# Lightning attention and a gated FFN on one core: the order of two transposes, of eight stores and of the state's decay

## The chip, the core and the metric

The kernel runs on one core of a Trainium2 chip. Five engines work side by side: TensorE (PE) does the matrix products, VectorE (DVE) and ScalarE (ACT) the elementwise work, GpSimd (POOL) issues the loads, SyncE (SP) issues the transposing transfers and the stores. Each engine takes its own instructions in order, and semaphores order work between engines. The metric is the device time of one execution in microseconds (us), as the median of seven runs. Beside it stands one execution that the profiler recorded.

## What is computed

Linear attention with a decay per head, over 4 sequences, 8 heads, 768 positions and 64 features, taken block by block; its output is the input of a gated FFN:

```python
for b in range(nb):                      # blocks of the sequence
    intra = einsum('bhic,bhjc->bhij', qb, kb) * Dmask[None]      # lam ** (i - j), lower triangle
    intra = einsum('bhij,bhjd->bhid', intra, vb)
    inter = einsum('bhid,bhde->bhie', qb * lam_pow[None], kv_state)
    out[:, :, sl] = intra + inter
    kb_dec = kb * rev_pow[None]
    kv_state = lam_block * kv_state + einsum('bhsd,bhse->bhde', kb_dec, vb)

x = out.transpose(0, 2, 1, 3).reshape(3072, 512)
y = (sigmoid(x @ w_gate) * (x @ w_val)) @ w_out      # d_ff = 1536
```

Inputs and output are float32; the kernel works in bfloat16 with float32 accumulators.

## The kernel before, in words

**Blocks.** The kernel takes 128 positions at a time: six blocks, n = 0 to 5, each of all 4 sequences and 8 heads. The FFN of a block has 12 tiles of the hidden width. For each tile `piece_gv` (line 488) runs four matmuls of the gate product into `gp` and four of the value product into `vp`, ACT takes the sigmoid of `gp` into `sg` (line 500), and DVE multiplies it with `vp` into `ht` (lines 503 and 505). `gp` and `vp` share three PSUM buffers. After the tiles, `piece_po` (line 522) makes the output rows of the four sequences, ACT copies each to `ob` (line 526), and SP stores it (line 512).

**Attention of the next block.** While the FFN of block n runs, the attention of block nx = n + 1 is prepared between its tiles. The order is written out by hand: `plan` is a list of units, `more[i]` is the list of pieces that follow tile i, and the program's text order is each engine's own order. For nx = 2 and later, the pieces are `e_q` (DVE: q transposed, times its decay, into `QS`, line 277), `chunk_s` (PE: scores, which reads `QS` and the transposed k, line 387), `chunk_m` (DVE: mask, line 397), `kd` (ACT: k times its decay, line 127, four groups of two heads), `decayed` (DVE: the state times its decay, into `XD`, line 456), `chunk_c` (PE: the state's increments from `kd` and v, line 447), `update_0` and `update_1` (DVE, lines 464 and 472), and after the last tile `att` (PE: the block's output, lines 411 and 425). `chunk_c` stands behind tile 8. In the FFN of block 1 most of these stand one tile later than in that of blocks 2 to 4 (`late`).

**Loads and transposes.** `next_loads(n)` has three steps. `xbar(n)` lets SP issue two transposing transfers, from `kb` to `KT` and from `qb` to `QT` (line 298), which wait for the three k loads and the three q loads of the block. `gate(n)` is a pair of tiny copies on POOL (line 615), which read the last elements of `KT` and `QT`, and so hold POOL until both transposes have landed. Then POOL issues v of block n and k and q of block n + 1 (lines 94 and 100), k ahead of q. Blocks 2 and 3 have their calls in the FFN of block 1, behind tiles 2 and 8; those of blocks 4 and 5 stand in the last output unit of blocks 1 and 2. The k and q of block 2 are loaded with blocks 0 and 1's data, before the first call.

**Stores of block 0.** Its output rows are copied to `ob` before block 1's FFN begins, but `piece_po` does not store them (`if n:`). They are stored by eight transfers of half rows that are listed behind a tile of block 1's FFN.

Of the kernel before, what the change touches and what calls it, by code (L numbers as in the profile page):

```python
# [16 lines left out]
def kernel(  # L17
# [242 lines left out]
    QT, KT = {}, {}  # L260
# [32 lines left out]
        nc.vector.tensor_copy(T_[c, 0][:, b], H32[c, b])  # L293

    def xbar(n):
        for c, d in (("k", KT), ("q", QT)):
            d[n] = qtp.tile([128, B, HP, C], BF16, tag=c + "t", name=c + "t")
            nc.sync.dma_start_transpose(  # L298
                out=d[n].rearrange("p b hp s -> p (b hp) s"),
                in_=T_[c, n].rearrange("p b h d -> p (b h d)"))  # L300
        for b in range(B):
            KS[n, b] = KT[n][:, b]
# [208 lines left out]
    def store(n, tt, c0=0, c1=DM):  # L511
        (nc.scalar if (n, tt, c1) == (NSTEP - 1, B - 1, DM) else nc.sync).dma_start(out=out[tt * S + n * C:tt * S + (n + 1) * C, c0:c1],
                          in_=OB[n, tt][:, c0:c1])
# [103 lines left out]
    def next_loads(n):  # L617
        xbar(n)
        gate(n)
        load(n, "v")  # L620
        if n + 1 < NSTEP:
            load(n + 1, "kq")
# [8 lines left out]
    def gv(n, ft, *more):  # L631
        unit(lambda: piece_gv(n, ft), *more)

    def po(n, tt, *more, c=(0, DM), eng=nc.scalar, fts=range(NFT)):
        unit(lambda: piece_po(n, tt, *c, eng, fts), *more)
# [16 lines left out]
    def do(f, *args, **kw):  # L652
        return lambda: f(*args, **kw)
# [4 lines left out]
    def att(n):  # L658
        def block():
            piece_i(n)  # L660
            piece_a(n, range(B))
            piece_x(n, range(B))
            for bp in range(2):
                piece_c(n, bp)

        def chunks():
            new_xt(n)
            for c, bp in A + Z:
                new_op(n, c, bp)
            done = [chunk_i(n, banks) for banks in (A, Z)]  # L670
            for name, banks in zip(done, (A, Z)):
                in_order(name)
                chunk_a(n, banks)
                for c, bp in banks:
                    chunk_x(n, c, bp)
        return block if n < FIRST_XBAR else chunks

    def kd(n, h0, h1=None, **kw):
        return do(piece_kd, n, range(h0, h1 or h0 + 2), **kw)
# [20 lines left out]
    for n in range(1, NSTEP):  # L700
        nx = n + 1
        more = [[] for i in range(NFT)]
        if nx < NSTEP:
            late = 1 if n == 1 else 0
            cs = (0, 1) if nx < NSTEP - 1 else (0,)
            for bp in range(2):
                more[2 + late + bp].append(do(e_q, nx, [2 * bp, 2 * bp + 1]))
                more[4 + late].append(do(chunk_s, nx, bp))
                more[8].append(do(chunk_c, nx, bp, cs))
            for bp in range(2):  # L710
                more[4 + late + bp].append(do(chunk_m, nx, bp))
                more[8].append(do(update_0, nx, bp))
                if 1 in cs:
                    more[9 + bp].append(do(update_1, nx, bp))
            more[6 + late].append(do(decayed, nx))
            more[3 + late].insert(0, do(make_kd, nx))
            for i in range(4):
                more[3 + late + i].append(kd(nx, 2 * i))
            more[11].append(att(nx))
        if n == 1:  # L720
            more[0].append(chunk_lamq)
            more[2].append(lambda: next_loads(2))
            more[3].extend([lambda tt=tt, j=j: store(0, tt, 256 * j, 256 * j + 256)
                            for tt in range(B) for j in range(2)])
            more[8].append(lambda: next_loads(3))
        for ft in range(NFT):
            gv(n, ft, *more[ft])
        for tt in range(B):
            if n == NSTEP - 1 and tt == B - 1:
                po(n, tt, c=(0, 384), eng=nc.vector)  # L730
                po(n, tt, c=(384, 512))
            else:
                more = [lambda n=n: next_loads(n + 3)] if tt == B - 1 and n + 3 < NSTEP else []
                po(n, tt, *more)
# [35 lines left out]
```

## Time and profile before

| | |
|---|---|
| median of 7 runs | 227.17 us (227.04 to 227.89) |
| profiled execution: its time, its span | 227.45 us, 225.7 us |
| granted TensorE clock | 1.0 of full speed |
| busy: TensorE, its weight loads | 216.2 us, 105.9 us |
| busy: VectorE, ScalarE, GpSimd | 104.2 us, 106.4 us, 63.9 us |
| FFN products: gate, value, output | 74.2 us (296 recorded), 74.1 us (292), 63.3 us (292) |
| transposes of k and of q, issue to landing | 4.5 to 6.5 us, 4.7 to 4.9 us (four of each) |
| v loads of 512 KB, issue to landing | 8.6, 8.0, 7.3 and 6.9 us (blocks 2 to 5) |

How to read it. The span runs from the first to the last recorded event of the profiled execution; its own time is 1.75 us longer. Busy time is the time in which an engine works on an instruction; waiting on a semaphore is not in it. The chain that ended last starts from the last instruction and goes back, at each step, to what released it or to the instruction before it on its engine: it is the list of things that set the end. The list of waits tells which engine waited at which line for whom. For a transfer the profile has two times: the interval in which an engine or a queue issues it, and the time from issue to landing. Numbers behind an L are line numbers of the kernel.

### The profile page before, as it was taken

How to read it: one execution, taken by the hardware profiler on the slowest of the kernel's cores; microseconds unless marked ns; L12 is line 12 of the kernel's file. 1: busy time of each engine (PE TensorE's matmuls, PEld its weight loads, DVE VectorE, ACT ScalarE, POOL GpSimd, SP SyncE). 2: the span in 40 equal slices, each digit the busy share in tenths (PEclk: the TensorE clock that was granted, in tenths of full speed). 3: DMA queues.
4: the chain of work that ended last, by engine and by line, in shares of the span. 5: the costliest groups of instructions: out<-in, count | busy, mean ns of one | idle time of the engine just before them, and what ended most of it. 6: DMA issues, size and time to landing. Idle time of an engine off the chain costs nothing.

```text
span 225.7 us, 5200 instructions
## 1 busy us (share of the span) xinstructions
PE 216.2 (96%) x2178; PEld 105.9 (47%) x2187; DVE 104.2 (46%) x196; ACT 106.4 (47%) x232; POOL 63.9 (28%) x83
## 2 busy tenths in 40 slices
PE   7699999999997999999999999999999999999994
PEld 2454444557443544444544444544444454444443
DVE  4785553539478800478800378800378500333300
ACT  5777534494374342385342385342385342333221
POOL 7998855660085008400930030000000000000000
PEclk9999999999999999999999999999999999999999
DMA  7999999999989998998999839012100012100022
GB/s 113 149 161 184 196 203 180 172 154 137 169 196 166 141 206 99 208 166 144 74 157 195 178 62 90 3 49 93 46 3 0 0 52 94 46 0 0 4 93 94
DMA packets 106008, 25.25 MB, mean 112 GB/s; under 512 B 97152, under 2 KB 103552, under 8 KB 105984
## 3 DMA queue, kind: packets, MB, share of 16 engines
q0 software_dynamic: 82944, 13.90, 86.0%
q1 hardware_dynamic: 22752, 10.95, 20.2%
q8 instruction: 17, 0.28, 0.5%
q10 hardware_dynamic: 288, 0.07, 0.1%
q14 instruction: 7, 0.06, 0.1%
HBM read 28.32 MB, written 6.29 MB: 153 GB/s over the span
## 4 chain that ended last, share of the span: by engine, by line
PE 67%; DMA 23%; POOL 6%; issue 2%; SPq 1%; ACT 0%; POOLq 0%
PE po L522 23%; PE gp L488 20%; PE vp L488 20%; DMA WO<-in_moe_w_out_dram 6%; DMA kb<-in_k_dram 4%; DMA vb<-in_v_dram 4%; DMA WV<-in_moe_w_val_dram 4%; DMA WG<-in_moe_w_gate_dram 3%; DMA qt<-qb 2%; SPq L298 1%; POOL vb L94 1%; PE cp L447 1%; PE op L411 1%; PE op L425 1%; POOL WG L105 1%
## 5 line engine op out<-in xcount | busy, mean ns | idle before, releaser
L488 PE MATMUL gp<-XT,WG 128*128 128x512 bf16 (+1 forms) x296 | 74.2, 374 | 0.2 <-DMA WG<-in_moe_w_gate_dram 0.2
L488 PE MATMUL vp<-XT,WV 128*128 128x512 bf16 (+1 forms) x292 | 74.1, 376 | 0.0
L500 ACT ACTIVATE sg<-gp 128x512 bf16<-128x512 f32 x72 | 43.0, 597 | 64.8 <-PE gp L488 61.4
L505 DVE TENSOR_TENSOR ht<-sg,vp 128x512 bf16<-128x512 bf16 x48 | 33.0, 687 | 79.9 <-PE vp L488 79.9
L522 PE MATMUL po<-WO,ht 128*128 128x512 bf16 (+2 forms) x292 | 63.3, 370 | 0.5 <-issue 0.2
L488 PEld LDWEIGHTS <-WV 128*128 128x128 bf16 x292 | 28.6, 98 | 33.4
L522 PEld LDWEIGHTS <-ht 128*128 128x128 bf16 x300 | 28.3, 98 | 31.9
L488 PEld LDWEIGHTS <-WG 128*128 128x128 bf16 x296 | 28.1, 98 | 32.1 <-DMA WG<-in_moe_w_gate_dram 0.9
L526 ACT COPY ob<-po 128x512 f32<-128x512 f32 (+1 forms) x24 | 13.7, 572 | 38.9 <-PE po L522 38.9
L127 ACT ACTIVATE kd<-kb,kds 128x128 bf16<-128x128 bf16 (+1 forms) x88 | 28.8, 401 | 0.0
L503 DVE TENSOR_TENSOR ht<-sg,vp 128x512 bf16<-128x512 bf16 x24 | 16.5, 686 | 13.0 <-PE vp L488 13.0
L615 POOL COPY gates<-kt 128x1 bf16<-128x1 bf16 x4 | 0.7, 186 | 51.2 <-DMA kt<-kb 51.2
L94 POOL DMA_DIRECT2D vb<-in_v_dram x9 | 11.9, 1332 | 2.6 <-issue 1.7
L318 DVE TENSOR_TENSOR MT<-sp,mask 128x512 bf16<-128x512 f32 x16 | 9.9, 684 | 3.0 <-PE sp L310 3.0
L437 ACT CAST XT<-op 128x512 bf16<-128x512 f32 x16 | 8.2, 599 | 5.0 <-PE op L425 5.0
L397 DVE TENSOR_TENSOR MT<-sp,mask 128x512 bf16<-128x512 f32 x16 | 10.3, 682 | 0.0
L100 POOL DMA_DIRECT2D qb<-in_q_dram x10 | 8.9, 911 | 2.5 <-DMA WO<-in_moe_w_out_dram 2.5
L100 POOL DMA_DIRECT2D kb<-in_k_dram x10 | 8.8, 894 | 1.9 <-DMA WO<-in_moe_w_out_dram 0.7
L94 POOL DMA_DIRECT2D qb<-in_q_dram x8 | 9.0, 1125 | 1.1 <-POOLq L754 0.8
L536 PE MATMUL zps<-st 128*128 128x512 bf16 x17 | 6.4, 509 | 1.6 <-DVE st L159 1.5
L94 POOL DMA_DIRECT2D kb<-in_k_dram x6 | 6.9, 1158 | 1.6 <-DMA WO<-in_moe_w_out_dram 1.1
L108 POOL DMA_DIRECT2D WV<-in_moe_w_val_dram x9 | 6.9, 766 | 1.0 <-DMA WG<-in_moe_w_gate_dram 0.6
(81 smaller groups left out, 114.2 us busy)
## 6 DMA issues: line engine op xcount, KB each, us to landing
out_dram<-ob SPq DMA_DIRECT2D x19, 256.0 KB, 2.1
vb<-in_v_dram POOLq DMA_DIRECT2D x4, 512.0 KB, 7.6
qb<-in_q_dram POOLq DMA_DIRECT2D x6, 256.0 KB, 10.1
kb<-in_k_dram POOLq DMA_DIRECT2D x6, 256.0 KB, 8.3
qb<-in_q_dram POOLq DMA_DIRECT2D x12, 128.0 KB, 9.4
WO<-in_moe_w_out_dram POOLq DMA_DIRECT2D x4, 384.0 KB, 12.3
kb<-in_k_dram POOLq DMA_DIRECT2D x10, 128.0 KB, 9.6
WG<-in_moe_w_gate_dram POOLq DMA_DIRECT2D x4, 256.0 KB, 7.4
```

What stands on the lines that cost most here:

```text
L94: nc.gpsimd.dma_start(out=T_[c, n][:, b0:nat], in_=src[b0:nat, :, sl, :].rearrange("b h s d -> s (b h) d"))
L100: nc.gpsimd.dma_start(out=T_[c, n][:, m:b1, u::2, :], in_=src[m:b1, 1 - u::2, sl, :].rearrange("b h s d -> s (b h) d"))
L127: nc.scalar.mul(KD[n][:, at, i, :], T_["k", n][:, at, i, :], kds[:, min(n // FIRST_XBAR, 1), h:h + 1])
L318: nc.vector.tensor_tensor(out=MT[n, b][:, u], in0=SP[n, b][u], in1=mask0[:, 1 - u if swapped(n, b) else u], op=ALU.mult)
L397: nc.vector.tensor_tensor(out=MT[n, bp][:, u], in0=SP[n, bp][u], in1=mask[:, u ^ bp].unsqueeze(1).to_broadcast([128, 2, HP, L]), op=ALU.mult)
L437: nc.scalar.copy(XT[n][:, c, :, bp * C:(bp + 1) * C], OP[n, c, bp].rearrange("p h j i -> p h (j i)"))
L488: nc.tensor.matmul(ps[:, part], lhsT=W[:, mt, fs], rhs=XT[n][:, part, mt], start=(part is not second and mt == 0), stop=(part is not first ...
L500: nc.scalar.activation(sg, gp.rearrange("p a b -> p (a b)"), AF.Sigmoid)
L503: nc.vector.tensor_mul(HT[n, ft], sg, vp.rearrange("p a b -> p (a b)"))
L505: nc.vector.tensor_mul(HT[n, ft].rearrange("p (b c i) -> p c b i", b=B, c=2), sg.rearrange("p (c b i) -> p c b i", c=2, b=B), vp.rearrange ...
L522: nc.tensor.matmul(po[:, :c1 - c0], lhsT=HT[n, ft][:, tt * 128:(tt + 1) * 128], rhs=WO[:, ft, c0:c1], start=(ft == 0), stop=(ft == NFT - 1))
L526: (eng.copy if eng is nc.scalar else eng.tensor_copy)(o, po[:, :c1 - c0])
```

## The change

Three edits, all to the order of things; no instruction is added or removed.

1. `xbar` issues the transpose of q before that of k, in each of the four blocks that use it. The gate copies and the loads keep their order.
2. The eight stores of block 0 move from the list behind tile 3 of block 1's FFN to that behind tile 6.
3. `decayed` moves from behind tile 6 to behind tile 0 in the FFN of blocks 2 to 4, and from behind tile 7 to behind tile 2 in that of block 1. `make_kd` and the four `kd` groups, which stood behind tiles 3 to 6 in blocks 2 to 4 and behind tiles 4 to 7 in block 1, now stand behind tiles 4 to 7 in all of them.

```diff
     def xbar(n):
-        for c, d in (("k", KT), ("q", QT)):
+        for c, d in (("q", QT), ("k", KT)):
             d[n] = qtp.tile([128, B, HP, C], BF16, tag=c + "t", name=c + "t")
             nc.sync.dma_start_transpose(
...
             late = 1 if n == 1 else 0
             cs = (0, 1) if nx < NSTEP - 1 else (0,)
+            more[2 * late].append(do(decayed, nx))
             for bp in range(2):
                 more[2 + late + bp].append(do(e_q, nx, [2 * bp, 2 * bp + 1]))
                 more[4 + late].append(do(chunk_s, nx, bp))
...
-            more[6 + late].append(do(decayed, nx))
-            more[3 + late].insert(0, do(make_kd, nx))
+            more[4].insert(0, do(make_kd, nx))
             for i in range(4):
-                more[3 + late + i].append(kd(nx, 2 * i))
+                more[4 + i].append(kd(nx, 2 * i))
             more[11].append(att(nx))
         if n == 1:
             more[0].append(chunk_lamq)
             more[2].append(lambda: next_loads(2))
-            more[3].extend([lambda tt=tt, j=j: store(0, tt, 256 * j, 256 * j + 256)
+            more[6].extend([lambda tt=tt, j=j: store(0, tt, 256 * j, 256 * j + 256)
                             for tt in range(B) for j in range(2)])
             more[8].append(lambda: next_loads(3))
```

## The prediction, made blind

> **What bounds the kernel now.** I read the page's busy time first, then the chain that ended last, then the waits, and last the timelines of SP, POOL, DVE and PE around the one place where the chain leaves TensorE. Busy time and the chain's shares on the page:
>
> ```profile
> PE 216.2 (96%) x2178; PEld 105.9 (47%) x2187; DVE 104.2 (46%) x196; ACT 106.4 (47%) x232; POOL 63.9 (28%) x83
> ...
> PE 67%; DMA 23%; POOL 6%; issue 2%; SPq 1%; ACT 0%; POOLq 0%
> ```
>
> TensorE is busy nearly throughout, so only a step that makes it wait longer or shorter moves the end. In order of time the chain runs over DMAs up to 71.9 us, and from there to the end over PE without a gap (columns: start us, length us, what):
>
> ```profile
> 44.84 9.78 DMA kb<-in_k_dram
> ...
> 54.71 3.29 SPq L298
> ...
> 58.10 4.69 DMA qt<-qb
> ...
> 62.84 0.19 POOL gates L615
> ...
> 63.28 8.62 DMA vb<-in_v_dram
> ...
> 71.95 0.73 PE cp L447 x61
> ```
>
> This is block 2's preparation: its k lands at 54.62, SP issues k's transpose and then q's, q's lands at 62.79, the gate copies on POOL let v's load go at 63.28, and v lands at 71.91, where PE stands before chunk_c (line 447). The waits say what PE loses in block 1's FFN (us in total, times, longest):
>
> ```profile
> PE cp L447 <- DMA vb<-in_v_dram: 1.4, 1, 1.4
> PE sp L387 <- DVE QS L277: 0.4, 1, 0.4
> ```
>
> So the v wait ends last: whatever delays v's landing delays the end one for one. SP's timeline shows the transposes and stores:
>
> ```profile
> 54.71 3.29 SPq L298 DMA_TRANSPOSE kt<-kb  x1
> 58.10 3.06 SPq L298 DMA_TRANSPOSE qt<-qb  x1
> 61.22 4.01 SPq L512 DMA_DIRECT2D out_dram<-ob  x8
> ...
> 124.86 1.98 SPq L298 DMA_TRANSPOSE kt<-kb  x1
> 127.07 2.10 SPq L298 DMA_TRANSPOSE qt<-qb  x1
> ```
>
> The last pair (block 5) runs with no load in flight, the first beside q's loads. And POOL's timeline, when block 2's q is loaded and the gates pass:
>
> ```profile
> 46.98 1.76 POOL L100 DMA_DIRECT2D qb<-in_q_dram  x2
> 61.31 0.19 POOL L615 COPY gates<-kt 128x1 bf16<-128x1 bf16 x1 [12.58 <-DMA kt<-kb]
> 62.84 0.19 POOL L615 COPY gates<-qt 128x1 bf16<-128x1 bf16 x1 [1.35 <-DMA qt<-qb]
> ```
>
> **What the Trainium skill says.** "DMA: Bandwidth & Descriptors", section "Issuing engines are not separate DMA queues": transfers issued from different engines run on the same DMA engines and interleave. The trace agrees: a 512 KB v load takes 8.6 us beside the eight stores (block 2) and 6.9 us alone (block 5). The same page, "Latency and other measured facts", gives a DMA transpose 261 GB/s; block 2's transposes move 128 x 2048 x 2 bytes = 524 KB each, an estimate of 2.0 us. Undisturbed, block 5's 1.98 and 2.10 us of issue agree; beside loads the trace has 3.3. "Perfetto Trace Analysis", section "DMA Instruction — HWDGE (DVE, Sync)": the profile's interval of such an instruction is not the data's movement. Here too: q's transpose is issued in 3.06 us but lands after 4.69, so I count landings.
>
> **The change, part by part.**
>
> *Stores of block 0, moved from the list behind FFN tile 3 to that behind tile 6.* I compared the order of instructions on each engine in both kernels. On SP the eight stores still stand between block 2's two transposes and block 3's; SP executes in its own order, and nothing that it issues lies between tiles 3 and 6. Their waits are on the same engines and lanes. Cost 0, as nothing moves. If they did come behind v's load, v could come nearer to its 7.3 us of block 4, 1.3 us of gain; I give that little chance.
>
> *q's transpose ahead of k's, in each block.* POOL loads k and then q, so SP now waits for q first. q's last load is the second of the pair at 46.98: issued at 46.98 + 0.88 = 47.86, and the DMA view gives 9.9 us to landing: 57.7. k's landed at 54.62. So the first transpose starts at 57.8 (0.09 after the landing, as k's did) and not at 54.71: 3.1 late. Part comes back. From the first start to the second landing, the pair took 8.1 us in block 2 (54.71 to 62.79), 8.0 in block 3 (76.81 to 79.89 + 4.9) and 8.3 in block 4 (98.19 to 101.65 + 4.8), each beside q loads still in flight; in block 5, with none, 6.9 (124.86 to 127.07 + 4.7). The swapped pair starts when the loads are over, so I take 6.9 and keep 8.1 as the other end: k's transpose lands at 57.8 + 6.9 = 64.7, against 62.79 before. Gates: k's copy waits for the last landing and q's runs behind it, so 0.2 us is added to the 0.49 from landing to v's issue: v goes at 65.4, against 63.28. Stores: SP is through with the pair after 127.07 + 2.10 - 124.86 = 4.3 us, so they go at 62.1 to 66.1, and cover 0.7 us of v's load instead of 65.23 - 63.28 = 1.95. v took 8.6 with them, 8.0 in block 3 with part of block 1's stores, 7.3 in block 4 and 6.9 with nothing beside; I take 8.2. v lands at 65.4 + 8.2 = 73.6, against 71.91: **+1.7 us**. The ends: 57.8 + 6.9 + 0.5 + 6.9 = 72.1 (+0.2), and 57.8 + 8.1 + 0.7 + 8.6 = 75.2 (+3.3).
>
> What queues behind this on the other engines: DVE's e_q needs only qt, which lands at about 62.4 (57.8 + 4.6), no later than 62.79; so DVE is not held longer. chunk_s on PE needs kt, at 64.7. PE is through with tile 5 at 63.9, waits 0.8 to 0.9 us, but no longer 0.4 for the second QS: it reaches chunk_c some 0.3 us later, at 70.9, and waits there until 73.6, 2.7 us instead of 1.4. The early wait is inside the v delay and is not added.
>
> Later blocks are covered. Block 3's q lands near 79.5 (its last load at 69.85 plus 9.5) against k's 76.8: with POOL's 2 us of lateness the pair starts at 81.6 and lands by 89.7 even at 8.1; v(3) goes at 90.4 and lands at 98.4 with 8.0 us. It is needed by chunk_c at 105.9 + 1.7, and the transposes by e_q at 95.6 + 1.7: 6 us or more of cover. Blocks 4 and 5 have more: their pairs landed at 106.5 and 131.8 for e_q's at about 129 and 163. If a cover were gone, the cost would be the whole lateness, 2 to 5 us a block. Stores of blocks 1 and 2 queue on SP behind these transposes, a few us late, for buffers that are wanted a block (34 us) later.
>
> *State decay (decayed, line 456) from tile 6 to tile 0, in block 1 from tile 7 to tile 2.* One instruction of 1.22 us per block, four in all, same count. In the FFN of blocks 2 to 4 the new place is between ht of tile 0 and of tile 1 (in block 1 between tiles 2 and 3), where DVE waits 1.04 us for PE: the next ht comes at most 0.2 late, and the accumulator that it frees is wanted by the gate product two tiles on, 1 us later. The old place also made PE wait nowhere: the chain runs over gp and vp rows of 0.86 us without a gap. Gain 0, cost 0, as slack covers both.
>
> *k's decay (kd) from tiles 3 to 6 to tiles 4 to 7, in the FFN of blocks 2 to 4.* Four ACT groups of 1.26 us a block. Block 1 had tiles 4 to 7 already: there the last group ended at 69.7, before the end of tile 8's value product at about 70.5. ACT needs 0.49 + 1.26 = 1.7 us a tile beside PE's 1.73, so it keeps pace. The cover is about 0.8 us a block; the order shows three new waits for ACT on chunk_c's weight loads in each of these blocks, met by then. Cost 0; gone, it would be up to 0.4 us a block.
>
> Sum: +1.7 us on the profiled execution's span, 225.7 to 227.4. That execution took 227.45 us, 1.75 around its span, 0.28 above the median 227.17; on the median: 227.17 + 1.7 = **228.9 us**.
>
> **The rivals.** (A) No relief: transposes and v keep their disturbed prices; v lands at 75.2, 230.4 us. For it: block 2's q transpose started after q's last landing and still took 3.06 us to issue; against: it ran behind k's slow one. (B) Not slower: relief in full. Transposes that begin after the loads and a v load past the stores run at their undisturbed prices, v lands at 72.1 and the time is 227.4. It decides when the pair, the gates and v take under 14.6 us together from 57.8 (72.36 is 0.45 behind 71.91); the fastest in the trace sum to 14.3, but block 3's loads follow v at once, as in block 4, where v took 7.3. A q landing before 57 without k's transposes beside it would push the same way. (C) The stores do go behind v: v takes 7.3, 228.0. Against: SP's order. (D) kd at its new place stalls chunk_c in blocks 2 to 4, 0.4 us each: 228.9 + 1.2 = 230.1. Against: block 1.
>
> **Numbers.** The forecast (+0.9 to +2.6) has 0.62, A 0.17, B 0.11 (of it 0.03 faster), C 0.04, D 0.06. About 0.2% (0.45 us) is what a measurement of this kernel can tell from no change. Slower by more: 0.62 + 0.17 + 0.04 + 0.06 = 0.89; within: 0.08; faster: 0.03. The range 227.9 to 230.5 leaves out B (0.11) and little of A and D beyond +3.3.
>
> **What would show it.** Right: on SP, q's transpose starts at about 57.8 and issues in near 2.1 us; the stores follow the pair; v's load goes at 65 to 65.5; PE waits 2.5 to 3 us for v before chunk_c, waits for kt before chunk_s, and shows no new gap after 75 us. Wrong: q's transpose starts before 57; stores come behind v; v lands before 72.4; or PE waits in blocks 2 to 4.

## The result, and the profile after

The changed kernel took 230.81 us (median of 12 executions, 228.88 to 232.33) against 227.35 us for the kernel before (31 executions): a ratio of 1.0141, with a 95% interval of 1.0124 to 1.0159. The forecast was 228.9 with a range to 230.5. The direction and the place were right; the size was not.

The execution that was profiled took 228.88 us, with a span of 227.1 against 225.7. It is one of only two in twelve whose mean TensorE clock was 1.000; the other ten have 0.976 to 0.993. The two took 228.88 and 229.31 us, the ten a median of 231.0. (A second set of six executions, below, took 229.86 us by the median, as only three of them had the low clock. How often the clock falls sets the median.) So there are two questions: what makes the profiled execution 1.4 us longer, and what adds another 1.9 us in most of the others.

The first is answered by the same views as before. The chain that ended last, in order of time (start us, length us, what), in the profile of the changed kernel:

```profile
47.44 9.99 DMA qb<-in_q_dram
...
57.50 2.05 SPq L298
...
59.66 4.71 DMA kt<-kb
...
64.42 0.31 POOL gates L615 x2
...
64.86 8.36 DMA vb<-in_v_dram
...
73.26 0.73 PE cp L447 x60
```

The chain now runs through q's load in place of k's. The first transpose starts at 57.50 instead of 54.71, the pair lands at 64.37 instead of 62.79, and v at 73.22 instead of 71.91. (This trace runs 0.4 us ahead of the earlier one up to here: tile 0 of block 1's FFN starts at 53.10 instead of 53.47. On TensorE's own scale v is 1.7 us later.) The waits in the stretch of block 1's FFN, 54 to 92 us (us in total, times, longest):

```profile
PE cp L447 <- DMA vb<-in_v_dram: 2.8, 1, 2.8
...
PE sp L387 <- DMA kt<-kb: 0.8, 1, 0.8
```

TensorE waits 2.8 us for v instead of 1.4, and 0.8 for k's transpose instead of 0.4 for the second QS: 1.8 us more. SP's timeline:

```profile
57.50 2.05 SPq L298 DMA_TRANSPOSE qt<-qb  x1
59.66 2.55 SPq L298 DMA_TRANSPOSE kt<-kb  x1
62.26 4.20 SPq L512 DMA_DIRECT2D out_dram<-ob  x8
```

The eight stores still follow the pair at once and begin before v's load (64.86), as the order of instructions had said; the last of them is issued at 66.46, so they run beside the first 1.6 us of that load. The page of this profile shows a full clock from end to end:

```profile
PEclk9999999999999999999999999999999999999999
```

So this profile can't show the second loss; the experiments have to.

### The profile page after: what moved, and what is told of

Its sections match the earlier page's. It is cut to its first block, busy times and chain, and to the rows that moved or that the text cites. A ratio compares the mean times of both kernels' runs of the same rounds, so it can differ in the third digit from the quotient of the medians.

```text
span 227.1 us, 5198 instructions
## 1 busy us (share of the span) xinstructions
PE 216.6 (95%) x2178; PEld 106.2 (47%) x2187; DVE 104.3 (46%) x196; ACT 106.4 (47%) x232; POOL 63.7 (28%) x83
## 4 chain that ended last, share of the span: by engine, by line
PE 66%; DMA 23%; POOL 7%; issue 2%; SPq 1%; ACT 0%; POOLq 0%
PE po L522 23%; PE gp L488 20%; PE vp L488 19%; DMA WO<-in_moe_w_out_dram 6%; DMA qb<-in_q_dram 4%; DMA vb<-in_v_dram 4%; DMA WV<-in_moe_w_val_dram 4%; DMA WG<-in_moe_w_gate_dram 3%; DMA kt<-kb 2%; POOL qb L94 1%; POOL vb L94 1%; PE cp L447 1%; PE op L411 1%; PE op L425 1%; POOL WG L105 1%
## 5 line engine op out<-in xcount | busy, mean ns | idle before, releaser
L505 DVE TENSOR_TENSOR ht<-sg,vp 128x512 bf16<-128x512 bf16 x48 | 33.0, 687 | 79.9 <-PE vp L488 76.9
L615 POOL COPY gates<-kt 128x1 bf16<-128x1 bf16 x4 | 0.7, 186 | 62.1 <-DMA kt<-kb 62.1
L536 PE MATMUL zps<-st 128*128 128x512 bf16 x17 | 7.0, 551 | 1.6 <-DVE st L159 1.5
```

The lines of the kernel that those rows point to most:

```text
L505: nc.vector.tensor_mul(HT[n, ft].rearrange("p (b c i) -> p c b i", b=B, c=2), sg.rearrange("p (c b i) -> p c b i", c=2, b=B), vp.rearrange ...
```

## The experiments

Ratios and differences are to executions of the kernel before that ran beside each kernel. "Low clock" means a mean TensorE clock under 0.997 in that execution's record; "full clock" is the rest. A stretch at half clock is called cold. A low mean is not enough by itself: in three of the profiles below the clock was at 0.50 for 3.4 us between 8 and 12 us, where the chain runs over loads, and these executions took an ordinary 226.72, 227.59 and 227.75 us. So I go by clock and time together.

**The swap alone**, on the kernel before:

```diff
-        for c, d in (("k", KT), ("q", QT)):
+        for c, d in (("q", QT), ("k", KT)):
```

> The kernel before with the swap of the two transposes alone. Theory (the swap makes block 2's v late by 1.4 us, and the longer idle time of TensorE before chunk_c then costs it part of its clock in most executions, about 1.7 us more): the whole loss, +3.2 us (1.014 of before), the granted clock near 0.993 in most executions. Rival 1 (the other edits, the decay or the kd groups, bring the low clock): +1.5 us and a clock of 1.000. Rival 2 (the low clock belongs to the chip or the hour, not to the kernel): a low clock beside the kernel before as well.

Measured: 230.36 us (9 executions), ratio 1.0100 (1.0067 to 1.0134). Four executions at a full clock had a median of 229.2, five with a low clock one of 230.5. In its profile TensorE waited 2.8 us for v. The swap alone brings both parts of the loss, so rival 1 is out; of the 53 executions of the kernel before beside it, 3 were long with a low clock, so the chip or the hour (rival 2) does not explain 5 of 9. How often the clock falls differs (5 of 9 here, 10 of 12 in the changed kernel), and so the ratio does.

**Everything but the swap**: the changed kernel with k first again.

> The changed kernel with k's transpose put back ahead of q's; the stores, the decay and the kd groups stay at their new places. Theory: as before within 0.2%, clock 1.000, a wait of 1.4 us for v. Rival 1 (the decay or the kd groups cost something or bring the low clock): +1.5 to +2 us. If the stores' new place did act, v would land earlier and the time would be up to 1.3 us shorter.

Measured: 227.35 us (20 executions), ratio 0.9997 (0.9976 to 1.0017), with a wait of 1.5 us for v. The stores, the decay and the kd groups cost and bring nothing that the interval (about 0.2% either way) would show. One execution of the 20 reached 229.8; the kernel before has such executions too (below).

**The wait filled with work**: the changed kernel with ten products that nobody reads, behind tile 8 of block 1's FFN.

```diff
+    def fill(m):
+        fp = ps_at.tile([128, DM], FP32, name="fill", tag="ps")
+        for _ in range(m):
+            nc.tensor.matmul(fp, lhsT=WO[:, 0, 0:128], rhs=WO[:, 0], start=True, stop=True)
...
+                if n == 1 and bp == 0:
+                    more[8].append(do(fill, 10))
                 more[8].append(do(chunk_c, nx, bp, cs))
```

> The changed kernel with ten products of 128x512 that nobody reads added on TensorE between tile 8 of block 1 and chunk_c (10 x 0.216 = 2.2 us), inside the wait of 2.8 us for v. Theory (idle time costs the clock): the clock is 1.000 in all executions and the time falls to +1.5 us over before (1.0065), though work was added. Rival (the clock falls for another reason, or the whole loss is lateness of v): +3.2 us as the changed kernel, or more by up to 2.2.

Measured: 228.98 us (18 executions, none above 229.85), ratio 1.0076 (1.0060 to 1.0092). TensorE's timeline in its profile (start us, length us, what; in brackets the idle time before and what ended it):

```profile
70.26 2.32 PE L684 MATMUL fill<-WO 128*128 128x512 bf16 x10
72.94 0.73 PE L447 MATMUL cp<-vb,kd 64*64 64x64 bf16 x64 [0.35 <-DMA vb<-in_v_dram]
73.60 1.04 PE L488 MATMUL gp<-XT,WG 128*128 128x512 bf16 x4
```

v is as late as in the changed kernel and chunk_c waits for it all the same, but the idle time before it is 0.35 us. With more work the kernel is 1.8 us faster by the medians (0.9 against the second set of the changed kernel), and the slower group of executions is gone: none of 18 here, where the swap alone, on the same chip, had 5 of 9. What is left, +1.7 us, is the lateness of v.

**The changed kernel again**, to look for the place where the clock falls.

> The changed kernel once more, unaltered, to see where the clock falls. Theory: the time is bimodal, about 228.9 us where the clock stays at 1.000 and about 230.6 where it is near 0.992; in a profile of the second kind the TensorE clock is low in the stretch that follows the wait for v (73 to 77 us), matmuls there take twice their time, and the rest is as in the first profile. Rival (the clock falls elsewhere): the low stretch lies at another place.

Measured: 229.86 us (6 executions), ratio 1.0098 (1.0064 to 1.0133); again two groups, 229.1 (three, clock 0.998 to 1.000) and 230.8 (three, 0.984 to 0.993). The profiled execution is of the first group and doesn't show the place. Those of the next two kernels do.

**Four products in place of ten** in the wait.

> The changed kernel with four unread products (0.9 us) in place of ten between tile 8 and chunk_c, so that about 1.9 us of idle time is left. Theory: 1.4 us of idle time left the clock alone in the kernel before and 2.8 took it in most executions, so this lies between: low clock in at most a third of the executions, median +1.6 to +2.2 us over before. Rival (idle time is not the cause): as the changed kernel, +3.2 us.

Measured: 230.29 us (4 executions only), ratio 1.0123 (1.0066 to 1.0179): two executions at 231.1 and 231.3, two at 228.6 and 229.5. So 2.4 us of idle time can be enough. Four executions cannot tell a half from the third that I had expected, and the interval holds both the theory's time and the rival's; what this kernel settles is the place. Its profiled execution is one of the long ones (231.34 us). Busy time by stretch in it (stretch; its length; busy us of PE, PEld, DVE, ACT, POOL; TensorE clock; DMA share; GB/s):

```profile
73.00:74.00 1.00, 0.00 (x0) 0.00 (x0) 0.00 (x0) 0.00 (x0) 0.00 (x0) 0.99 2.38 164
74.00:75.00 1.00, 0.90 (x64) 0.90 (x63) 0.21 (x1) 0.00 (x0) 0.00 (x0) 0.50 2.44 152
75.00:76.00 1.00, 1.00 (x18) 0.39 (x7) 1.00 (x2) 0.00 (x0) 0.00 (x0) 0.50 2.43 155
76.00:77.00 1.00, 1.00 (x4) 0.39 (x3) 0.07 (x1) 0.00 (x0) 0.00 (x0) 0.50 2.47 157
77.00:78.00 1.00, 1.00 (x5) 0.39 (x4) 0.00 (x0) 0.60 (x1) 0.00 (x0) 0.80 2.58 155
```

And TensorE's timeline there:

```profile
74.10 1.07 PE L447 MATMUL cp<-vb,kd 64*64 64x64 bf16 x64 [2.41 <-DMA vb<-in_v_dram]
75.11 1.89 PE L488 MATMUL gp<-XT,WG 128*128 128x512 bf16 x4
76.79 1.33 PE L488 MATMUL vp<-XT,WV 128*128 128x512 bf16 x4
77.96 1.03 PE L488 MATMUL gp<-XT,WG 128*128 128x512 bf16 x4
```

The clock is halved at the end of the wait and comes back at 77.4: 3.4 us at half speed, which is 1.7 us of work lost. The first gate product after the wait takes 1.89 us instead of 1.03. This is the second loss, at the place that the theory named. No long execution of the changed kernel itself was profiled; that its loss lies at the same place follows from the counts with and without the wait, not from a trace.

**A long wait without a swap**: the kernel before with chunk_c of block 2 behind tile 7 instead of 8, and the kd groups a tile earlier. (The expectation says that update_0 moves as well; in the kernel that ran it stayed behind tile 8.)

```diff
-                more[8].append(do(chunk_c, nx, bp, cs))
+                more[8 - late].append(do(chunk_c, nx, bp, cs))
...
-                more[3 + late + i].append(kd(nx, 2 * i))
+                more[3 + i].append(kd(nx, 2 * i))
```

> The kernel before (k's transpose first) with chunk_c and update_0 of block 2 one tile earlier in block 1's FFN, behind tile 7, and the kd groups one tile earlier with it. v lands at 71.9 as before, PE reaches chunk_c at 68.8 and waits 3.1 us, and one tile more (1.73 us) stands behind the wait. Theory: +1.7 us from the tile and about +1.7 from the clock in most executions: median +3.4, clock near 0.992, without any swap of transposes. Rival (the low clock comes with the swapped transposes and not with the wait): +1.7 us and a clock of 1.000.

Measured: 231.40 us (4 executions), ratio 1.0176 (1.0140 to 1.0212), all four with a low clock (0.985 to 0.993). Its TensorE timeline:

```profile
72.15 1.07 PE L447 MATMUL cp<-vb,kd 64*64 64x64 bf16 x64 [3.46 <-DMA vb<-in_v_dram]
73.16 1.89 PE L488 MATMUL gp<-XT,WG 128*128 128x512 bf16 x4
```

A wait of 3.5 us with k's transpose first halves the clock just the same (0.50 until 75.5, again 3.4 us). The tile that now stands behind the wait is 1.7 of the +4.0 us and the half clock another 1.7; the profiled execution, 230.83 us, has just these 3.4. The further 0.6 of the median is not explained. The low clock belongs to the wait, not to the transposes.

**q loaded first as well**: the changed kernel with the order of POOL's loads swapped too.

```diff
-    load(2, "kq")
+    load(2, "qk")
...
-            load(n + 1, "kq")
+            load(n + 1, "qk")
```

> The changed kernel with q loaded ahead of k on POOL for blocks 2 to 5, so that the transpose that is first on SP is again that of the load that lands first. Theory (the swap costs because q is loaded last, and not because q's transpose goes first): as before within 0.3%, q's transpose starts at about 54.7 us, v goes at 63.3 to 63.5, the wait for v is 1.2 to 1.7 us, clock 1.000. Rival (k's transpose last makes chunk_s and kd late on its own): +0.5 us or more, as PE waits for kt before chunk_s and kd for k's load.

Measured: 227.54 us (20 executions), ratio 1.0028 (1.0005 to 1.0051). SP's timeline:

```profile
54.80 3.28 SPq L298 DMA_TRANSPOSE qt<-qb  x1
58.18 3.08 SPq L298 DMA_TRANSPOSE kt<-kb  x1
```

The pair stands where it stood before, and v's load goes at 63.37. Thirteen executions with a clock of at least 0.998 had a median of 227.2, beside 227.43 for the kernel before. The swap of the transposes is not what makes v late; that the first of them waits for the load that lands last is. TensorE no longer waited before chunk_s and so idled 2.0 us before chunk_c instead of 1.4, more than the 1.2 to 1.7 expected, and in 7 of 20 executions the clock fell (228.8 to 229.9 us): that accounts for the ratio's 0.28%. The ratio alone would allow the rival's +0.5 us; against it stand the full-clock executions and the wait before chunk_s that is gone.

**chunk_c one tile later**, on the kernel before:

```diff
-                more[8].append(do(chunk_c, nx, bp, cs))
+                more[8 + late].append(do(chunk_c, nx, bp, cs))
...
-                more[8].append(do(update_0, nx, bp))
+                more[8 + late].append(do(update_0, nx, bp))
...
-                    more[9 + bp].append(do(update_1, nx, bp))
+                    more[9 + late + bp].append(do(update_1, nx, bp))
```

> The kernel before with chunk_c, update_0 and update_1 of block 2 one tile later in block 1's FFN (behind tiles 9 to 11). Theory (v's landing at 71.9 ends the wait, PE reaches chunk_c at 70.6): PE comes there at 72.3, the wait of 1.4 us is gone, and the time is 1.4 us shorter (0.994 of before). Rival (something else is late then, the updates for the attention behind tile 11): 0 to -0.5 us, with a new wait behind tile 11.

Measured: 226.01 us (15 executions), ratio 0.9939 (0.9924 to 0.9953): faster than both kernels, and no wait for v is left among the waits of that stretch. The wait of 1.4 us was worth about 1.4 us of the kernel's time.

**The same on the changed kernel:**

> The changed kernel with chunk_c, update_0 and update_1 of block 2 one tile later in block 1's FFN (behind tiles 9 to 11). v lands at 73.2 as in the changed kernel, PE reaches chunk_c at 72.1 and waits 1.1 us. Theory (lateness of v plus a clock that is lost with the long wait): both go, the time is -0.3 us against before (0.999), clock 1.000; that is 3.5 us less than the changed kernel for 1.73 us of work moved into the wait. Rival (only the lateness counts): 1.73 us less than the changed kernel, 1.006 of before.

Measured: 227.66 us (12 executions), ratio 1.0003 (0.9976 to 1.0031), with a wait of 1.3 us. Moving 1.73 us of work into the wait brings 3.15 us by the medians (230.81 to 227.66): the wait and, in all but one execution, the halved clock with it. The rival's 1.006, reckoned from the ratio 1.0141, is outside the interval; reckoned from the second set's 1.0098 it would be 1.002 and inside. The count decides: 1 long execution with a low clock of 12, against 13 of 18 of the changed kernel.

**Both orders swapped, and chunk_c one tile later:**

> The changed kernel with q loaded ahead of k on POOL for blocks 2 to 5, and chunk_c and the updates of block 2 one tile later. Theory: v lands near 72, PE reaches chunk_c at about 72, no wait, clock 1.000: 0.993 to 0.994 of before, at or a little under the kernel before with chunk_c one tile later, as the 0.4 us that chunk_s waited for the second QS may go. Rival (the transposed k, last now, holds chunk_s longer): 0.996.

Measured: 225.74 us (4 executions), ratio 0.9923 (0.9905 to 0.9941), the fastest of all; v lands at 71.70 there and TensorE takes chunk_c at once:

```profile
63.17 8.53 DMA vb<-in_v_dram
...
71.74 0.73 PE cp L447 x61
```

Against the kernel before with chunk_c later (0.9939) the intervals overlap, so the last 0.3 us is not settled.

**Without block 0's stores**, on the kernel before:

> The kernel before without the eight stores of block 0 (the output rows of block 0, a sixth of the output, are not written), to price what the stores cost v's load and what hiding them behind it could have brought. If the stores are what makes v take 8.6 us: v takes about 7.3 as in block 4, lands at 70.6, and the time is 1.2 us shorter (0.995). If the k and q loads of block 3 behind it are: 8.4 to 8.6 us and a time within 0.3 us of before.

Measured: 226.65 us (10 executions), ratio 0.9962 (0.9950 to 0.9974). v took 7.6 us instead of 8.6 and the wait for it fell to 0.4. So the stores do cost v about 1 us, between the two expectations. Leaving them out altogether brought 0.8 us; what putting them behind v would bring was not tried.

**The swap in blocks 3 to 5 only:**

> The kernel before with q's transpose first in blocks 3 to 5 alone; block 2 keeps k first. Theory (the loss is all in block 2, later blocks are covered): within 0.2% of before, clock 1.000, v of block 3 2 to 3 us later than before with no wait for it. Rival (lateness carried on by SP and POOL costs in later blocks): +0.5 us or more, with new waits after 95 us.

Measured: 227.60 us (12 executions), ratio 1.0014 (1.0001 to 1.0027), with no wait of TensorE for a load after 90 us in its profile. v's load of block 3 goes at 87.08 us instead of 85.55 and nothing waits for it. The interval just reaches the rival's +0.5 us, so if the later blocks cost anything, it is within 0.3%; block 2 is the place of the loss.

**How often the clock falls.** Counting the executions that are both long (by 1 us or more over their own kernel's group at full clock; where there is no such group, all of the low ones) and low in clock, by the idle time before chunk_c in the kernel's profile, which is that of one execution:

| idle time before chunk_c (kernels) | executions with the loss |
|---|---|
| 0 to 0.4 us (chunk_c later; ten products; both swapped and later; no stores) | 0 of 47 |
| 0.7 us (blocks 3 to 5 swapped; its profile is its shortest execution, 0.9 us under the median) | 0 of 12 |
| 1.3 to 1.5 us (before; all but the swap; changed with chunk_c later) | 6 of 139 |
| 2.0 us (q loaded first as well) | 7 of 20 |
| 2.4 us behind four products | 2 of 4 |
| 2.5 to 2.8 us (changed, twice; swap alone) | 18 of 27 |
| 3.5 us (chunk_c earlier) | 4 of 4 |

The Trainium skill describes a mechanism: "TensorE: Matmul & The Clock Gate", section "What's actually happening", says that a monitor halves TensorE's clock after about one idle window of 3.4 us and gives it back after such a window of work, and that the window runs freely, whatever the kernel does. The trace agrees on the half (0.50) and on the 3.4 us of cold work. It does not agree that a whole window must be idle: 2.4 us took the clock in the profile above, and a kernel whose profile idled 2.0 us lost it in a third of its executions. Nor must the idle time be in one piece: in the profile of the changed kernel with chunk_c later, the early cold stretch (8.3 to 11.7 us) comes after two waits of 0.5 and 1.3 us, with work between them. That the fraction grows with the idle time fits a window that falls differently in each execution; that link is argued and not shown.

## Why the prediction was right or wrong, point by point

**What bounds the kernel: right.** v's landing ends the wait before chunk_c. Taking that wait away brought 0.6% (chunk_c later).

**The stores don't move: right.** SP issues them between the pairs, at 62.26, where 62.1 was forecast; rival C is out. They run beside 1.6 us of v's load, where 0.7 was forecast. The gain of 1.3 us from stores behind v was set too high: without stores v took 7.6 us, not 7.3. Of the difference between 8.6 and 6.9 us, which the prediction puts down to the stores, they are thus about 1.0.

**The swap: right in mechanism, and near in size.** The first start was forecast 3.1 us late and was 2.8 (3.2 with the 0.4 us by which the trace was ahead). The pair took 6.87 us (forecast 6.9), gates and issue 0.49 us (0.7: the second copy on POOL follows the first within 0.12, so that nothing was added), v 8.36 us (8.2). The wait for v was 2.8 us (2.7), that for k's transpose 0.8. Executions at full clock stood at 229.1 us, where 228.9 was forecast. Rivals A and B, disturbed or undisturbed prices throughout, are out: v landed at 73.22, not at 75.2 or 72.1. That A's 230.4 us is near the measured median is luck. (The prediction set its estimate of 2.0 us for a transpose beside issue intervals of 1.98 and 2.10 us, which by its own reading are not the data's movement; these two landed 4.5 and 4.7 us after issue. Its sum rightly used landings.)

**The step that failed** is the sentence "whatever delays v's landing delays the end one for one". It took an idle microsecond on TensorE for a microsecond. With 2.4 us or more of idle time before chunk_c, 24 of 35 executions were also long with a low clock; where a trace shows it, TensorE runs at half its clock for 3.4 us, a term of 1.7 us that the sum did not have. The mean clock of 1.0 in the profile of before could not show it, as the wait there was 1.4 us; but the forecast itself had a wait of 2.7 us, nearly twice as long as any in that trace, and did not ask what that would do. None of the rivals named the clock. The range's upper end (230.5) came from prices of transfers and was passed by 0.3 us.

**Decay and kd: right.** All but the swap gives 0.9997, and among the waits after 92 us in the changed kernel's profile none is of TensorE's products, so rival D is out. That profile puts three of DVE's waits before `ht`, 2.9 us in all, down to ACT's kd groups, but DVE lost nothing by them: its waits at line 505 sum to 79.9 us in both profiles, and the first of the three (0.97 us, at 105.69) has its match before (0.97 us, at 106.10), put down to TensorE there. One sum is off: 0.49 + 1.26 is 1.75 us a tile, not 1.7. By the start times before (61.46, 61.95, 63.18) a tile takes ACT 1.72 us, just under TensorE's 1.73, so ACT keeps pace with nothing to spare.

**Later blocks: right.** Swapped alone they give 1.0014, with no new wait of TensorE.

## What to carry to other kernels

When a change lengthens a wait of TensorE, price the wait twice: its own length, and what the clock may do after it. Here a wait of 1.4 us cost about 1.4 us, and kernels with a wait of 2.5 to 2.8 us paid, in 18 of 27 executions, for the half clock as well (1.3 to 1.9 us by the medians of the groups); a profile that happened to keep its clock shows only the first part, so look at the clocks of all executions. And what goes first on a queue should be what lands first: what the swap of the transposes cost, a like swap of the loads took back. Moving the waiting work one tile back brought more still: the kernel before became 0.6% faster.

## What the runs showed of the hardware that was not expected

- 2.4 us of idle time on TensorE was followed by 3.4 us at a clock of 0.50, and so was 3.5 us of idle time; 2.8 us in the profile of the changed kernel was not. It is a matter of chance per execution, with the fractions in the table above.
- Ten products without a reader in the wait (2.3 us in the trace) made the kernel faster, by 1.8 us against the first set of the changed kernel and 0.9 against the second, and no execution of 18 lost its clock there.
- In six profiles the swapped pair of block 2 starts after the loads have landed. It lands 6.8 to 7.4 us after its start, against 8.1 beside loads in the profile of before. The time to issue its first transpose varies more, from 2.0 to 3.0 us, against 3.3 beside loads.
- In three profiles the clock was halved for 3.4 us after a wait of 1.3 to 1.4 us and a shorter one of 0.4 to 0.5, early in the execution, where it cost no time that shows.
